# Chunked delta-rule attention with two MLP layers: first joins 64 rows at a time, a PSUM tile per engine in the first copies, low weight parts by GpSimd, ks of chunk 1 ahead of y

## The chip, the core and the metric

One Trainium2 chip, one of its cores. The metric is the device time of one execution in microseconds (us). The engines are named as in the profile: PE is TensorE's matmuls, PEld its weight loads, DVE is VectorE, ACT is ScalarE, POOL is GpSimd, SP is SyncE, which here issues nearly all DMAs.

## The reference

```python
def _attn_ref(q, k, v, beta):                 # (4, 8, 768, 48): batch, heads, tokens, head size
    k_n = k / (np.linalg.norm(k, axis=-1, keepdims=True) + 1e-06)
    state = np.zeros((B, H, D, D)); y = np.zeros_like(q)
    for t in range(S):
        kt, vt, bt = k_n[:, :, t], v[:, :, t], beta[:, :, t, None]
        y[:, :, t] = einsum('bhd,bhde->bhe', q[:, :, t], state)
        v_old = einsum('bhde,bhd->bhe', state, kt)
        state = state + bt[:, :, :, None] * einsum('bhd,bhe->bhde', kt, vt - v_old)
    return y
def _moe_ref(x, w_in, w_out):                 # 3072 tokens, 384 -> 2048 -> 384
    h = x @ w_in
    return np.where(h > 0, h, np.exp(np.minimum(h, 0)) - 1) @ w_out
def _moe2_ref(x, w_in, w_out):
    h = x @ w_in
    return (h / (1 + np.exp(-1.702 * h))) @ w_out
# reference: _moe2_ref(_moe_ref(attention as (3072, 384)))
```

All in float32.

## The kernel before, in words

**Attention.** The 768 tokens are cut into 12 chunks `c` of 64; two chunks make a pass `p`. The 32 sequences (4 batches, 8 heads) lie in two halves of the partitions, 16 each. Inside a chunk the token-by-token recurrence becomes a triangular system: `gram64` or `gram` multiplies the keys by themselves (into `z`), `inverse(p)` inverts the unit triangular 32x32 blocks on DVE (one step is a product, L318, and a sum, L323), `across` or the chunk's own `m1` and `m2` join the 32-blocks to 64. Passes 0 to 2 (`FINE`) run the steps on 16x16 blocks only, and `join16` joins two 16-blocks into a 32-block by two products on TensorE: `left` (L357, copied to `ys` by L359) and `right` (L368, subtracted by L371). Then a chunk runs `kq` (L455, masked by L466), `ks` (old state times keys, L513, subtracted from v by L518), `w` (L530), `state` (L549, copied by L765 and L767 in chunk 0, added by L556 later) and `y` (L574 and L584, split by L595 on ACT and L596 on DVE).

**MLP.** Every float32 operand is split into a high and a low word, and a product is three matmuls: high times high, high times low, low times high. A unit is one of 16 column blocks `m` of one pass of 512 tokens in one layer, 192 units in all. A unit `u` is `up` (9 matmuls of 128x128 by 128x512, L669), an activation (ACT L678 and L679, DVE L682), the split into `gh` (ACT L691) and `gl` (DVE L694), and, two units later, `down` (9 matmuls, L706). `up` needs a PSUM tile `h`, of which there are two: unit u waits until L682 of unit u-2 has read its own.

**Weights.** `prep` makes the two words of a weight tile out of its raw float32 form: a DMA, a power-of-two change on ACT (L628), `shift` (L635) and `rest` (L638) on DVE, `high` (L645, a cast on ACT) and `low` (L649, the difference of the bits and the high word, 128x768, on DVE). In layer 0 these run one or two units ahead of the unit that reads the tile.

**Order.** The kernel is scheduled by hand: each engine runs its instructions in the order of the program. `schedule` first writes out the prologue call by call: grams of chunks 0 and 1, whose copies out of PSUM (`diag`, L765 on ACT and L767 on DVE in turns, and `off`, L224 on ACT) fill `z`; the 16-steps of pass 0; grams of chunks 2 and 3; then the joins and the recurrences of chunks 0 and 1, with steps of pass 1 between (`also`). After `self.early = False` come the units. `fill`, `mid`, `end` and `tail` are tables by unit; in `fill` stands the weight preparation, and behind it the steps of later passes, which `spread` lays over the units by the room that `taken` leaves. Pass 2 has its steps in units 9 to 16.

**PSUM.** `ps_m` holds two `h` tiles and the three sums `acc0` to `acc2`, a bank each; `ps_a` holds `ps_w` (two banks in one tile, `wide()`) and one bank `ps_b`. `bank(True)` gives an `h` tile while `early` is set, `banks(i)` gives two of the sums.

Of the kernel before, what the change touches and what calls it, by code (L numbers as in the profile page):

```python
# [20 lines left out]
P = 128  # L21
# [11 lines left out]
class Kernel:  # L33
# [34 lines left out]
    def constants(self):  # L68
# [5 lines left out]
        self.ident = self.ap.tile([P, P], F32, name="ident")  # L74
        make_identity(nc, self.ident)
# [126 lines left out]
    def gram64(self, c, kt, ps):  # L202
# [10 lines left out]
        def diag(i, hf):  # L213
# [124 lines left out]

    def join16(self, c, home):
# [4 lines left out]
        own = {}  # L344

# [4 lines left out]
        def left(half):  # L350
# [3 lines left out]
            for u in range(8 * half, 8 * half + 8):  # L354
# [6 lines left out]
        def right(half):  # L361
# [3 lines left out]
            for u in range(8 * half, 8 * half + 8):  # L365
# [51 lines left out]
    def chunk(self, c):  # L417
# [123 lines left out]
        def state():  # L541
            if last:
                return
            ps = self.wide()
            for u in range(8):
                for hf, ab in self.order():
                    k = self.w_half(hf, ab)
                    t, r = self.tok(k), slice(64 * (1 - ab), 64 * (1 - ab) + D)
                    pe.matmul(ps[r, hf, ss(u)], g["kn"][t, hf, hs(u)], su[k][t, hf, ss(u)], start=True, stop=True)  # L549
            for hf, ab in self.order():  # L550
                k = self.w_half(hf, ab)
                r, q = [slice(64 * (1 - x), 64 * (1 - x) + D) for x in (k, ab)]
                if first:
                    self.evac(1 - hf, heads(nx[k][r, hf]), heads(ps[q, hf]))
                    continue
                v.tensor_tensor(out=heads(nx[k][r, hf]), in0=heads(su[k][r, hf]), in1=heads(ps[q, hf]), op=ALU.add)  # L556
# [49 lines left out]
    def prep(self, layer, ms, pools):  # L606
# [171 lines left out]
    def schedule(self):  # L778
# [66 lines left out]
        both = self.wide()  # L845
        diag0, off0, _ = self.gram64(0, self.grp[0]["kt"], [both[:, hf] for hf in range(2)])
        diag0(1, 0)
        self.load_q(0, gate=True)
        diag0(1, 1)
        diag1, off1, _ = self.gram64(1, self.grp[1]["kt"], self.banks(1))  # L850
        diag1(1, 0)
        diag1(1, 1)
        off0(0)
        off0(1)
        off1(0)
        off1(1)
# [6 lines left out]
        for f in first[0]:  # L863
            f()
        c0["kq"]()
        for c, kg in ((2, self.kg), (3, kg3)):
            both = self.wide()
            all_of = self.gram64(c, kg, [both[:, hf] for hf in range(2)])[2]
            all_of(0)
            all_of(1)  # L870
# [49 lines left out]
        for f in loads[4:6]:  # L920
            f()
        c0["y"]()
        c1["ks"]()
# [223 lines left out]
```

## Time and profile before

| | us |
|---|---|
| median of three runs (1002.73 to 1006.55) | 1005.05 |
| the profiled execution, as timed | 1009.37 |
| its span, first to last instruction | 1007.6 |
| PE busy in it | 952.0 |
| DVE busy | 598.0 |
| ACT busy | 444.6 |
| POOL busy | 49.4 |

The profile is of one execution. It gives each instruction's start and duration, groups them by line and shape, and puts an idle stretch of an engine down to the instruction that ended last before it (the releaser); "issue" means that the profile shows no releaser. Busy time of an engine is an average over stages: the first 75 us are attention alone, up to about 196 us the units share the engines with attention and weight preparation, and after that TensorE has almost no gaps.

### The profile page before, as it was taken

The numbers are of one execution on the slowest core, as the hardware profiler recorded it, in microseconds if no ns is written. First come the engines' busy times: TensorE is split into PE (matmuls) and PEld (weight loads), VectorE is DVE, ScalarE is ACT, GpSimd is POOL, SyncE is SP. The second block draws the span as 40 slices with busy tenths as digits, with TensorE's granted clock in tenths as the row PEclk, the third lists the DMA queues.
The fourth block names the chain that finished last, engine by engine and source line by source line (L and its number), as shares of the span: only waits on it lengthen the run. The fifth ranks groups of instructions, "written<-read, shape, count | busy, mean of one in ns | idle before, by whom it ended". The sixth has DMA issues, their size and how long they took to land.

```text
span 1007.6 us, 27118 instructions
## 1 busy us (share of the span) xinstructions
PE 952.0 (94%) x12288; PEld 780.1 (77%) x12288; DVE 598.0 (59%) x1054; ACT 444.6 (44%) x726; POOL 49.4 (5%) x55
## 2 busy tenths in 40 slices
PE   4678889899999999999999999999999999999998
PEld 3566667687877887888887888888888888888886
DVE  5969649857986888688344777744333333333333
ACT  5535455445345344444545776533333333333332
POOL 2100000001001001000000010100101001010000
PEclk9999889999999999999999999999999999999999
DMA  7144232402220321211101921001010010100000
GB/s 253 51 164 149 87 112 101 138 35 59 71 97 18 91 65 56 76 55 52 34 2 73 408 84 63 1 1 63 1 63 1 0 63 1 43 20 1 32 1 31
DMA packets 20180, 68.43 MB, mean 68 GB/s; under 512 B 3168, under 2 KB 4704, under 8 KB 20064
## 3 DMA queue, kind: packets, MB, share of 16 engines
q1 hardware_dynamic: 19920, 66.56, 19.1%
q8 instruction: 96, 1.57, 0.6%
q14 instruction: 20, 0.16, 0.1%
q10 hardware_dynamic: 144, 0.13, 0.0%
HBM read 57.25 MB, written 9.44 MB: 66 GB/s over the span
## 4 chain that ended last, share of the span: by engine, by line
PE 88%; DVE 8%; issue 3%; ACT 1%; DMA 0%; ACTq 0%; DVEq 0%
PE h L669 39%; PE acc L706 28%; PE accn L706 10%; PE ps_w L455 1%; PE ps_w L513 1%; PE ps_w L530 1%; PE ps_w L194 1%; PE ps_w L549 1%; PE ps_w L574 1%; PE ps_w L584 1%; DVE wt L649 1%; DVE tmp L318 1%; PE ps_b L368 1%; DVE W L323 1%; PE ps_w L408 1%
## 5 line engine op out<-in xcount | busy, mean ns | idle before, releaser
L669 PE MATMUL h<-xh,wt 128*128 128x512 f32 x1152 | 398.8, 401 | 6.3 <-DVE W L328 2.6
L706 PE MATMUL acc<-gh,wt 128*128 128x512 f32 x864 | 292.6, 393 | 0.5 <-DVE xo L767 0.5
L669 PEld LDWEIGHTS h<-xh,wt 128*128 128x128 f32 x1152 | 219.4, 191 | 56.2 <-DVE W L328 2.7
L669 PE MATMUL h<-xl,wt 128*128 128x512 f32 x576 | 227.8, 395 | 0.0
L691 ACT CAST gh<-t 128x512 fp32r<-128x512 f32 x192 | 119.4, 622 | 191.1 <-DVE t L682 134.9
L706 PEld LDWEIGHTS acc<-gh,wt 128*128 128x128 f32 x864 | 162.8, 188 | 35.9 <-issue 0.9
L694 DVE TENSOR_TENSOR gl<-t,gh 128x512 fp32r<-128x512 f32 x192 | 138.5, 722 | 71.5 <-ACT gh L691 71.3
L706 PE MATMUL acc<-gl,wt 128*128 128x512 f32 x432 | 168.7, 390 | 0.0
L688 DVE TENSOR_TENSOR t<-t,h 128x512 f32<-128x512 f32 x96 | 66.0, 687 | 168.8 <-ACT t L685 168.8
L685 ACT ACTIVATE t<-h 128x512 f32<-128x512 f32 x96 | 57.4, 598 | 187.3 <-PE h L669 187.3
L669 PEld LDWEIGHTS h<-xl,wt 128*128 128x128 f32 x576 | 110.0, 191 | 21.4
L682 DVE SCALAR_TENSOR_TENSOR t<-t,h 128x512 f32<-128x512 f32 x96 | 65.6, 683 | 79.6 <-ACT t L679 79.1
L678 ACT ACTIVATE t<-h 128x512 f32<-128x512 f32 x96 | 57.4, 598 | 98.1 <-PE h L669 97.9
L706 PE MATMUL accn<-gh,wt 128*128 128x512 f32 x288 | 96.5, 389 | 0.0
L706 PEld LDWEIGHTS acc<-gl,wt 128*128 128x128 f32 x432 | 81.5, 189 | 16.3
L706 PEld LDWEIGHTS accn<-gh,wt 128*128 128x128 f32 x288 | 54.1, 188 | 11.2
L679 ACT ACTIVATE t<-t 128x512 f32<-128x512 f32 x96 | 60.7, 632 | 3.1
L706 PE MATMUL accn<-gl,wt 128*128 128x512 f32 x144 | 56.0, 389 | 0.0
L733 POOL TENSOR_TENSOR xl<-x1r,xh 128x512 fp32r<-128x512 f32 x18 | 24.1, 1337 | 407.2 <-ACT xh L732 314.4
L466 DVE TENSOR_TENSOR x<-ps_w,mask_p 64x512 f32<-64x512 f32 x44 | 30.2, 687 | 9.7 <-PE ps_w L455 9.3
L638 DVE SCALAR_TENSOR_TENSOR w<-raw,w 128x768 uint32<-128x768 uint32 x32 | 33.7, 1053 | 0.9
L313 DVE TENSOR_TENSOR W<-W,tmp 128x30 f32<-128x30 f32 (+14 forms) x90 | 29.9, 332 | 3.1
(171 smaller groups left out, 804.4 us busy)
## 6 DMA issues: line engine op xcount, KB each, us to landing
raw<-in_w SPq DMA_DIRECT2D x32, 768.0 KB, 7.4
kt<-in_kT SPq DMA_DIRECT2D x12, 512.0 KB, 4.3
x<-in_qT SPq DMA_DIRECT2D x24, 256.0 KB, 4.1
kg<-in_kT SPq DMA_DIRECT2D x9, 512.0 KB, 4.8
kn<-in_kn SPq DMA_DIRECT2D x12, 384.0 KB, 3.0
x1d<-xo SPq DMA_DIRECT2D x12, 384.0 KB, 2.9
x1r<-x1d SPq DMA_DIRECT2D x6, 768.0 KB, 4.8
vn<-in_vn SPq DMA_DIRECT2D x11, 384.0 KB, 3.6
```

Source lines behind the costliest of these rows:

```text
L313: v.tensor_tensor(out=w, in0=w, in1=t, op=ALU.add)
L466: v.tensor_tensor(out=g["x"][k][self.tok(k), 8 * hf:8 * hf + 8], in0=i, in1=self.mask_p[t].unsqueeze(1).to_broadcast(list(i.shape)), op=AL ...
L638: v.scalar_tensor_tensor(out=bits[m], in0=words(m, 0), scalar=29, in1=bits[m], op0=ALU.logical_shift_right, op1=ALU.bitwise_or)
L669: nc.tensor.matmul(hps, wt[:, part, k * P:(k + 1) * P], src[:, k], start=(i == 0), stop=(i == 3 * NK - 1))
L678: nc.scalar.activation(out=t, in_=hps, func=AF.Relu, scale=-1.0)
L679: nc.scalar.activation(out=t, in_=t, func=AF.Exp, scale=-1.0)
L682: nc.vector.scalar_tensor_tensor(out=t, in0=t, scalar=-1.0, in1=hps, op0=ALU.add, op1=ALU.max)
L685: nc.scalar.activation(out=t, in_=hps, func=AF.Sigmoid, scale=1.702)
L688: nc.vector.tensor_tensor(out=t, in0=t, in1=hps, op=ALU.mult)
L691: nc.scalar.copy(gh, t)
L694: nc.vector.tensor_tensor(out=gl, in0=t, in1=gh.bitcast(F32), op=ALU.subtract)
L706: self.nc.tensor.matmul(self.acc[c], wt[:, part, DM + c * P:DM + (c + 1) * P], src, start=(m == 0 and i == 0), stop=(m == NM - 1 and i == 2),)
```

## The change

- `join16`: `left` for chunks 0 and 1 and `right` for chunk 1 multiply 64 rows at a time. The stationary operand is a 64x64 block-diagonal tile (`self.blocks`, two tiles of 128x1024, set to zero by POOL at the start), into which `block` copies the 16-blocks by four ACT copies of 32x16x16. A product of 16 heads is then 32 matmuls instead of 64.
- The first grams: chunk 0 uses two `h` banks instead of one two-bank tile; of each chunk's two tiles ACT copies one and DVE the other (`evac(1 - hf, ...)`), four copies each, where the two took turns on each tile. The `off` copies move behind the first four steps of pass 0 (`start`, `take`, `diag`, `root`), and chunk 3's gram gets banks of its own instead of `ps_w`.
- `state` of chunk 0 uses two `h` banks, one for ACT's and one for DVE's copies.
- `low` of layer 0 runs on POOL instead of DVE, and `taken` in its units is 0.37 instead of 0.6. The 16 `low`s of layer 1 stay on DVE.
- `ks` of chunk 1 stands ahead of `y` of chunk 0.
- The identity tile goes.

```diff
+        self.blocks = []
+        for c in range(2):
+            t = self.wp.tile([P, 2 * DM, 2], F32, name="raw", tag="wt").rearrange("p k i -> p (k i)")[:, 0:1024]
+            nc.gpsimd.memset(t, 0.0)
+            self.blocks.append(t.rearrange("p (u t) -> p u t", u=16))
...
-                    self.evac(i + far, z[r, :, 0:32], p[r, :, 32 * far:32 * far + 32])
+                    self.evac(1 - hf, z[r, :, 0:32], p[r, :, 32 * far:32 * far + 32])
...
+    def block(self, to, x):
+        for q in range(4):
+            r, i = slice(32 * q, 32 * q + 32), 32 * (q % 2)
+            self.nc.scalar.copy(to[r, :, i:i + 16], x[r, :, 0:16])
...
+        wide = [c < 2, c == 1]
+        def pairs(ps, x, half):
+            for u in range(8 * half, 8 * half + 8):
+                for o in (0, 64):
+                    r = slice(o, o + 64)
+                    pe.matmul(ps[r, u, :], own["d"][r, u, :], x[r, u, :], start=True, stop=True)
...
+            if wide[1]:
+                if half == 0:
+                    own["d"] = self.blocks[0]
+                    self.block(own["d"], own["t1"])
+                pairs(ps, own["ys"], half)
...
-            ps = self.wide()
+            if first:
+                ps = [self.bank(True) for _ in range(2)]
...
-            v.tensor_tensor(out=wt[:, 1], in0=bits.pop(m).bitcast(F32), in1=wt[:, 0].bitcast(F32), op=ALU.subtract)
+            (v if layer else nc.gpsimd).tensor_tensor(out=wt[:, 1], in0=bits.pop(m).bitcast(F32), in1=wt[:, 0].bitcast(F32), op=ALU.subtract)
...
-        for f in first[0]:
+        for f in first[0][:4]:
+            f()
+        for off in (off1, off0):
+            off(0)
+            off(1)
+        z = self.pas[0]["z"]
+        self.block(self.blocks[0], z[:, 0:16])
+        for f in first[0][4:-1]:
             f()
...
+        self.block(self.blocks[1], z[:, 16:32])
+        all3 = self.gram64(3, kg3, [self.banks(1)[1], self.bank()])[2]
...
+        c1["ks"]()
         c0["y"]()
-        c1["ks"]()
...
-            taken[m - 2] = 0.6
+            taken[m - 2] = 0.37
```

ACT's order at the very start, before; `acc_150` and `acc_151` are the two tiles of chunk 1's gram, `ps_w` that of chunk 0:

```order
L765 COPY z<-ps_w 32x8x32 x2
L155 COPY x_141<-one 128x1
L765 COPY z<-ps_w 32x8x32 x2
L765 COPY z<-acc_150 32x8x32 x2
L765 COPY z<-acc_151 32x8x32 x2
L224 COPY z<-ps_w 32x8x32 x4
L224 COPY z<-acc_150 32x8x32 x2
L224 COPY z<-acc_151 32x8x32 x2
L273 ACTIVATE nb<-dg 128x32
```

The same stretch of ACT after the change; `h` is chunk 0's first tile, `raw` the first block-diagonal tile:

```order
L793 COPY z<-h 32x8x32 x4
L157 COPY x_141<-one 128x1
L793 COPY z<-acc_150 32x8x32 x4
L275 ACTIVATE nb<-dg 128x32
L226 COPY z<-acc_150 32x8x32 x2
L226 COPY z<-acc_151 32x8x32 x2
L226 COPY z<-h 32x8x32 x4
L345 COPY raw<-z 32x16x16 x4
```

The square root (`nb`) moved ahead of the eight `off` copies, and four block copies follow them.

PE's order through the joins of chunks 0 and 1, before (L357 left, L368 right, L482 and L497 `m1` and `m2` of chunk 0):

```order
L357 MATMUL h<-xl,z 32x16 x64
L357 MATMUL ps_b<-xl,z 32x16 x32
L368 MATMUL h<-xh 32x16 x64
L357 MATMUL ps_b<-xl,z 32x16 x32
L482 MATMUL h<-z 32x32 x32
L368 MATMUL ps_b<-xh 32x16 x32
L497 MATMUL h<-xl,xh 32x32 x32
L368 MATMUL ps_b<-xh 32x16 x32
```

The same stretch after the change (L360 is the 64-row product, L392 the right product of chunk 0, L506 and L521 `m1` and `m2`):

```order
L360 MATMUL h<-xl,raw 64x16 x32
L360 MATMUL ps_b<-xl,raw 64x16 x16
L392 MATMUL h<-xh 32x16 x64
L360 MATMUL ps_b<-xl,raw 64x16 x16
L506 MATMUL h<-z 32x32 x32
L360 MATMUL ps_b<-xh,raw 64x16 x16
L521 MATMUL h<-xl,xh 32x32 x32
L360 MATMUL ps_b<-xh,raw 64x16 x16
```

The groups kept their places; 96 of 352 matmuls went. The last two L360 groups read a block tile that ACT fills between its copies of `m1` and of `m2`.

POOL's order from the start of the joins to pass 3, before (L490 and L399 clear parts of `z`, L263 masks `W` of an inverse):

```order
L490 MEMSET z 32x16x32 x4
L399 MEMSET z 32x32x32 x2
L263 AFFINE_SELECT W<-W 128x1024
L267 MEMSET W 128x16x16
L263 AFFINE_SELECT W<-W 128x1024
```

The same stretch after the change:

```order
L514 MEMSET z 32x16x32 x4
L677 TENSOR_TENSOR wt<-w,wt 128x768 x7
L423 MEMSET z 32x32x32 x2
L677 TENSOR_TENSOR wt<-w,wt 128x768 x5
L265 AFFINE_SELECT W<-W 128x1024
L269 MEMSET W 128x16x16
L677 TENSOR_TENSOR wt<-w,wt 128x768 x4
L265 AFFINE_SELECT W<-W 128x1024
```

Sixteen `low`s (L677) came to POOL; the masks and clears now stand in a row with them.

## Rows read from the trace of the kernel before

**Rows 1.** The page, busy time, share and instruction count of each engine.

```profile
PE 952.0 (94%) x12288; PEld 780.1 (77%) x12288; DVE 598.0 (59%) x1054; ACT 444.6 (44%) x726; POOL 49.4 (5%) x55
```

**Rows 2.** Stages: length, busy PE, PEld, DVE, ACT, POOL, granted clock, DMA.

```profile
75.00:92.50 17.50, 14.77 (x164) 10.37 (x164) 16.72 (x24) 8.81 (x15) 0.00 (x0) 0.90 0.43 147
92.50:150.00 57.50, 48.27 (x1394) 38.61 (x1393) 31.64 (x46) 30.30 (x51) 1.90 (x2) 0.88 0.32 108
150.00:196.00 46.00, 39.61 (x829) 31.60 (x827) 44.12 (x93) 24.04 (x38) 1.58 (x2) 1.00 0.41 131
196.00:1007.60 811.60, 805.50 (x8242) 659.47 (x8242) 452.60 (x770) 345.89 (x555) 35.44 (x29) 1.00 0.15 52
```

**Rows 3.** Timeline, first copies: start, length, instruction, [idle before <- releaser].

```profile
6.65 0.42 DVE L767 COPY z<-ps_w 32x256 f32<-32x256 f32 x1 [6.65 <-ACT z L765]
10.51 0.88 DVE L767 COPY z<-acc 32x256 f32<-32x256 f32 x2 [0.43 <-ACT z L765]
11.81 1.49 ACT L224 COPY z<-ps_w 32x256 f32<-32x256 f32 x4
12.28 1.90 DVE L257 STREAM_TRANSPOSE W<-z 128x1024 f32<-128x1024 f32 x1
14.47 1.27 POOL L263 TENSOR_SCALAR_AFFINE_SELECT W<-W 128x1024 f32<-128x1024 f32 x1 [8.70 <-DVE dg L262]
```

**Rows 4.** Timeline, joins to the first unit, 40 to 75 us.

```profile
40.39 0.42 DVE L371 TENSOR_TENSOR z<-xl,h 128x256 f32<-128x256 f32 x1
48.84 1.96 PE L530 MATMUL acc<-vn,z 64*64 64x48 f32 x64
56.47 1.12 DVE L767 COPY su<-ps_w 48x384 f32<-48x384 f32 x2 [1.50 <-ACT su L765]
57.11 0.66 PE L574 MATMUL h<-x,su 128*32 128x64 f32 x16
61.83 0.33 PE L584 MATMUL h<-x,su 128*32 128x64 f32 x4 [2.06 <-issue]
66.18 2.08 PE L530 MATMUL acc<-raw,z 64*64 64x48 f32 x64 [1.17 <-DVE raw L518]
74.77 0.80 PE L669 MATMUL h<-xh,wt 128*128 128x512 f32 x1 [0.98 <-DVE xl L596]
```

**Rows 5.** PE's waits in 75 to 200 us, and the instruction queue of the page.

```profile
PE ps_w L455 <- issue: 2.9, 1, 2.9
PE h L669 <- DVE W L328: 2.6, 1, 2.6
PE ps_w L194 <- ACT z L411: 2.2, 1, 2.2
PE ps_w L194 <- issue: 2.1, 1, 2.1
PE ps_w L408 <- issue: 2.0, 1, 2.0
PE h L669 <- DVE wt L649: 1.5, 1, 1.5
PE h L669 <- DVE t L682: 1.2, 1, 1.2
q8 instruction: 96, 1.57, 0.6%
```

**Rows 6.** A stretch of 2.5 us at the lower clock, columns as in rows 2.

```profile
117.50:120.00 2.50, 2.50 (x48) 2.19 (x43) 1.18 (x2) 0.00 (x0) 0.00 (x0) 0.50 0.02 7
```

**Rows 7.** POOL beside DVE in layer 1, the same DVE line alone, and `low`.

```profile
588.98 1.29 POOL L733 TENSOR_TENSOR xl<-x1r,xh 128x512 fp32r<-128x512 f32 x1 [6.86 <-ACT xh L732]
589.13 1.95 DVE L638 SCALAR_TENSOR_TENSOR w<-raw,w 128x768 uint32<-128x768 uint32 x1
78.82 0.96 DVE L638 SCALAR_TENSOR_TENSOR w<-raw,w 128x768 uint32<-128x768 uint32 x1
L649 DVE TENSOR_TENSOR wt<-w,wt 128x768 fp32r<-128x768 f32 x32 | 30.3, 951 | 0.0
```

More of the change, by code (lines that the diff above doesn't have):

```diff
@@ L7 @@
 from concourse import mybir
-from concourse.masks import make_identity
 F32 = mybir.dt.float32
@@ L353, in left @@
             ps = own["ps"]
-            for u in range(8 * half, 8 * half + 8):
+            if wide[0]:
+                own["d"] = self.blocks[c]
+                pairs(ps, s["zt"][:, us, 16:32], half)
+            for u in range(8 * half, 8 * half + 8 * (not wide[0])):
                 for q in range(4):
@@ L364, in right @@
             ps = own["ps"]
-            for u in range(8 * half, 8 * half + 8):
+            if wide[1]:
[3 more added lines that the diff above has]
+                pairs(ps, own["ys"], half)
+            for u in range(8 * half, 8 * half + 8 * (not wide[1])):
                 for q in range(4):
@@ L543, in state @@
                 return
-            ps = self.wide()
+            if first:
+                ps = [self.bank(True) for _ in range(2)]
+            else:
+                both = self.wide()
+                ps = [both[:, hf] for hf in range(2)]
             for u in range(8):
@@ L548, in state @@
                     t, r = self.tok(k), slice(64 * (1 - ab), 64 * (1 - ab) + D)
-                    pe.matmul(ps[r, hf, ss(u)], g["kn"][t, hf, hs(u)], su[k][t, hf, ss(u)], start=True, stop=True)
+                    pe.matmul(ps[hf][r, ss(u)], g["kn"][t, hf, hs(u)], su[k][t, hf, ss(u)], start=True, stop=True)
             for hf, ab in self.order():
@@ L553, in state @@
                 if first:
-                    self.evac(1 - hf, heads(nx[k][r, hf]), heads(ps[q, hf]))
+                    self.evac(1 - hf, heads(nx[k][r, hf]), heads(ps[hf][q]))
                     continue
-                v.tensor_tensor(out=heads(nx[k][r, hf]), in0=heads(su[k][r, hf]), in1=heads(ps[q, hf]), op=ALU.add)
+                v.tensor_tensor(out=heads(nx[k][r, hf]), in0=heads(su[k][r, hf]), in1=heads(ps[hf][q]), op=ALU.add)
         def y():
@@ L844, in schedule @@
         self.a_start(0)
-        both = self.wide()
-        diag0, off0, _ = self.gram64(0, self.grp[0]["kt"], [both[:, hf] for hf in range(2)])
-        diag0(1, 0)
+        diag0, off0, _ = self.gram64(0, self.grp[0]["kt"], [self.bank(True) for _ in range(2)])
+        diag0(0)
         self.load_q(0, gate=True)
-        diag0(1, 1)
+        diag0(1)
         diag1, off1, _ = self.gram64(1, self.grp[1]["kt"], self.banks(1))
[L851 to L856, printed above, removed]
+        diag1(0)
+        diag1(1)
         self.load_kg(2)
@@ L862, in schedule @@
         self.load_kg(3, kg3)
-        for f in first[0]:
+        for f in first[0][:4]:
[6 more added lines that the diff above has]
+        for f in first[0][4:-1]:
             f()
         c0["kq"]()
[L866 to L870, printed above, removed]
+        both = self.wide()
+        all2 = self.gram64(2, self.kg, [both[:, hf] for hf in range(2)])[2]
+        all2(0)
+        all2(1)
+        self.block(self.blocks[1], z[:, 16:32])
+        all3 = self.gram64(3, kg3, [self.banks(1)[1], self.bank()])[2]
+        all3(0)
+        all3(1)
+        first[0][-1]()
         self.load_v(0)
```

4 lines of the change are left out of this document (1 added, 3 removed).

## The prediction

> **What bounds the kernel now.** I read the page's busy line first, then stages, then timelines and waits inside the stages. TensorE (PE) is busy 94% of the span [rows 1], but unevenly: after 196 us it works 805.5 of 811.6 us, so there nothing but its own work counts, and it idles 2.7 us between 75 and 92.5, 9.2 from there to 150 and 6.4 from there to 196 [rows 2]. Up to 75 us PE runs only small products. The end moves by what the prologue (up to the first L669 at 74.77 [rows 4]) and the idle time between 75 and 196 us give back. Who is late differs: in 150 to 196 DVE is busy 44.1 of 46 us, in 92.5 to 150 only 31.6 of 57.5 [rows 2]. Between 75 and 200 us the largest single waits of PE are "issue": 2.9, 2.1 and 2.0 us before small products; one of 2.6 stands under DVE W L328 [rows 5]. In rows 4 L584 waits 2.06 us for "issue" as well.
>
> What "issue" is can be worked out. The instruction queue moved 96 packets, 1.57 MB [rows 5]; PE and PEld have 24,576 records [rows 1], which is 96 x 256. Counted along PE's program, each of these stalls begins at record 191 + 256k (k = 10 for L584, 16, 19 and 22 for the three, 31 for the 2.6). A float32 product of 48 columns takes four records, so small products use up 256 records in little more than a microsecond, faster than the next packet comes; among large products (0.2 us for two records, from 805.50 us for 8242 [rows 2]) nothing shows. So the number of PE instructions costs time, even where they are short. [...]
>
> **The change, part by part.** The profiled execution took 1009.37 us with a span of 1007.6, 4.3 above the median of 1005.05; I sum against the former and take the sum off the median.
>
> *First copies.* DVE's pair of 0.88 us waited 0.43 for ACT, and the transpose came at 12.28 [rows 3]. Its first copy began at 6.65, when ACT's first of about the same 0.42 was done, and one in two waited again. With a tile each, both engines start together at about 6.25, and eight DVE copies of 0.44 run without a partner: transpose at about 9.9, **-2.4**. I count nothing for the square root, moved ahead of the `off` copies (1.49 on ACT): the inverse starts from POOL's L263, which ends at 15.74 and is released by DVE's L262 [rows 3].
>
> *Joins.* 96 of 352 products go, but PE is not late there: the copies and subtractions on DVE are (L371 at 40.39 has no idle time of DVE before it [rows 4]). I cost PE's saving at 0; DVE's subtractions and masks hide it, and if they did not, 96 products of four records, some 1.3 us per 256 at best, would give up to 2. The block tiles are cleared by POOL, which idles for 8.70 us at that time [rows 3]. The identity tile and the other banks of chunk 3's gram cost nothing that is waited for. The four block copies (4 x 0.37 on ACT, from `off` at 1.49 for four) stand ahead of the copy of `m2`'s result and part of `right` of chunk 1. So of the 2.4 gained, w of chunk 0 (48.84 [rows 4]) keeps about 1.3.
>
> *State copies.* L767 waited 1.50 for ACT's half of one tile [rows 4]. With two banks that goes: L767 ends at about 54.7 instead of 57.59, **-2.9** including the 1.3.
>
> *ks ahead of y.* At 54.7 ks comes first, 64 products of 48 columns like L530's 1.96 us [rows 4], ending near 56.7. Behind it on PE stands y. It ran from 57.11 to about 63.05 (66.18 less the wait of 1.17 and ks's 1.96), 5.9 us with L584's stall of 2.06 [rows 4], so 3.9 of work, and a stall again if a packet boundary falls in it: end 60.6 to 62.6. Meanwhile DVE subtracts (L518), which before put 1.17 us on the path [rows 4] and now lies under y; at worst it waits for two `low`s on POOL (1.94 each, below) and ends at 60.6, so even that is covered. w of chunk 1 starts at 60.6 to 62.6 instead of 66.18, and needs as before 8.6 us to the first L669. That gives 3.6 to 5.6; with the two terms above in it, the prologue is worth **-4.7** (bounds -3 to -5.5; y's copies on ACT now wait behind ks).
>
> *Units 0 to 3 (75 to 92.5).* The wait for L649 (1.5) goes to POOL, which runs `low` right after the cast and 1.5 units before its use, and a part of L682's 1.2 [rows 5], since DVE, 16.7 of 17.5 us busy [rows 2], sheds 0.95 per `low`. With PE's idle time goes one half-clock stretch (1.7). DVE's chain gives 0.8 back. **-3.1** (-1 to -3.9).
>
> *Fetch stalls.* 384 records fewer, and two waits more, shift every later boundary by one and a half packets. Of the stretches of 256 records after it, those with small products alone stall some 2 us, that with 4 large ones about 1, with 14 about 0.5 (a large product fills 0.2 us, and beside 18 of them no stall showed). The list of after has one full stall (in L392 to L196), 1 and 0.5, and one that hides under the 2.2 us wait for L411; the 2.0 and the 2.6 [rows 5] have no counterpart. Before: 2.9 + 2.1 + 2.0 + 2.6 = 9.6; after: about 3.6 to 5.6, and a half-clock stretch less or more. **-4.0** (0 to -7).
>
> *150 to 196 us.* Here DVE ends last. Six `low`s (0.95 each [rows 7]) leave it, -5.7. But POOL's operations hold up DVE ones that read two operands from SBUF: L638 takes 0.96 alone and 1.95 beside a POOL operation of 1.29 that started 0.14 earlier [rows 7]. `low` on POOL, 768 columns instead of 512, takes an estimated 1.94. Five of them (units 9 to 13) would put 9.7 on DVE if all its operations were blocked; those that read PSUM are not, which spares some 0.4 each: +7.7. Net **+2.0** (-5.7 to +4). `taken` at 0.37 only moves six 16-steps from units 14 to 16 to 10 to 13. [...]
>
> *Units 0 to 8.* The same blocking, with DVE idle nearly half the time [rows 2]: **+0.5**. A `low` late on POOL would hold `shift` two units on; there are two units of slack. POOL's masks and clears stand behind `low`s but are due later. SP's loads of x for the second chunk wait for y as before, those of the keys move earlier; nothing waits for either.
>
> Sum: -4.7 - 3.1 - 4.0 + 2.0 + 0.5 = -9.3. 1009.4 becomes 1000.1, the median 1005.05 about **996**.
>
> **The rivals.** *The lock decides (slower).* Every one of the 14 `low`s up to unit 13 holds DVE for 1.94, where DVE is on the path throughout: 27.2 less the 13.3 that leave it is +13.9; PE's idle time behind it brings three half-clock stretches, +5.1. With -10.3 from prologue and fetch stalls the time is about 1013.5. For it: L638 doubles [rows 7], DVE is 44.1 of 46 busy. Against: in 92.5 to 150 DVE is idle 26 us [rows 2], and only part of its operations read SBUF twice. It decides from the point at which a `low` costs PE over 1.1 us net.
>
> *The stalls stay (same).* Boundaries fall on other small products, as long as before, and the half-clock stretches with them: the fetch term is 0, the rest -5.3, time about 1000; with the prologue at its lower bound 1002. For it: there are as many small products in units 1 to 9 as there were. Against: the counted list. [...]
>
> *No lock (faster).* DVE's work in these units reads PSUM or finds its gaps, as most POOL operations now pass without a trace of harm: term 150 to 196 at -5.2, units 0 to 8 at 0, sum -17, time 988. For it: POOL is 5% busy and has room. Against: rows 7.
>
> **How the numbers follow.** Forecast (994 to 999) 0.55; the lock 0.10; same 0.18; no lock 0.17. A measurement of this kernel tells about 0.5% (5 us) from no change. Faster by more than that, below 1000: the forecast and the no-lock case nearly whole, 0.70; slower, 0.10; the remainder of 0.20 is the rival at 1000 to 1002 and the forecast's upper end. The range goes from the no-lock case, 987, to 1005, past the same rival, and leaves out the lock and the tail of the no-lock case.
>
> **What would show it.** The transpose (L259) at about 9.9; the first L697 near 70; no 1.5 wait before DVE's state copy; POOL's L677 at 1.94 each and two-operand DVE operations stretched beside it in units 9 to 13; "issue" stalls at other lines than L455 and L408, and three or four half-clock stretches instead of five. A first L697 later than 72 shows the prologue wrong; DVE without a stretched operation shows the lock wrong; PE waits of 2 us for DVE in units 9 to 16 would show that its price is too small; stalls of the same sum fell the fetch term.

## The result, and the profile of the changed kernel

| | before | changed |
|---|---|---|
| median of five runs (lowest to highest), us | 1006.55 (1002.73 to 1014.42) | 996.09 (993.81 to 998.32) |
| profiled execution, as timed, us | 1009.37 | 997.16 |
| its span, us | 1007.6 | 995.4 |

The ratio is 0.9884, with a 95% interval of 0.9834 to 0.9934; a second set of runs (below, e9) gave 0.9879, 0.9865 to 0.9893. The kernel became faster by 1.2% (no change lies outside the interval), and 996.09 us stands beside the 996 of the forecast. The medians differ by 10.5 us, the two profiled executions by 12.2; the forecast's sum was 9.3. That it is so near is in part luck, as the parts show.

The page of the changed kernel: its busy line, and two groups of its costliest instructions (line, engine, operation, count, then busy us and mean ns of one).

```profile
PE 953.3 (96%) x12096; PEld 782.7 (79%) x12096; DVE 597.4 (60%) x1038; ACT 449.1 (45%) x738; POOL 81.3 (8%) x71
L666 DVE SCALAR_TENSOR_TENSOR w<-raw,w 128x768 uint32<-128x768 uint32 x32 | 38.3, 1196 | 0.9
L677 POOL TENSOR_TENSOR wt<-w,wt 128x768 fp32r<-128x768 f32 x16 | 30.5, 1912 | 66.9 <-ACT wt L673 66.8
```

Against [rows 1] PE has 192 matmul records and as many weight loads fewer, 384 together, as counted. (The two lists of PE's order in "The change" add up to 320 and 224 matmuls: 96 of 320 went, not of 352; nothing was worked out from the 352.) DVE has lost sixteen instructions of 0.95 us (16 x 0.95 = 15.2) and is busy for 597.4 instead of 598.0 us: most of the relief came back in other instructions (below, under e2).

To see where the time went, both traces are cut where the same work ends: before the first up product, after 293 matmul records of PE, after 1262 more, and where 8242 are left. Columns as in [rows 2]. The kernel before:

```profile
74.80:94.00 19.20, 16.47 (x293) 11.80 (x293) 18.38 (x26) 8.81 (x15) 0.00 (x0) 0.91 0.45 158
94.00:149.00 55.00, 45.77 (x1261) 36.57 (x1260) 29.41 (x42) 29.30 (x49) 1.90 (x2) 0.88 0.29 97
149.00:196.00 47.00, 40.61 (x846) 32.41 (x835) 44.89 (x94) 25.04 (x39) 1.58 (x2) 1.00 0.42 137
```

The changed kernel:

```profile
72.00:88.50 16.50, 14.20 (x293) 10.79 (x293) 15.51 (x22) 8.79 (x15) 4.97 (x3) 1.00 0.47 152
88.50:139.00 50.50, 44.87 (x1262) 35.48 (x1261) 30.79 (x38) 29.37 (x49) 12.72 (x9) 0.90 0.35 117
139.00:185.00 46.00, 42.10 (x832) 33.81 (x833) 42.12 (x87) 24.55 (x39) 12.69 (x8) 0.96 0.38 127
185.00:995.40 810.40, 804.02 (x8242) 657.79 (x8240) 454.01 (x771) 346.04 (x556) 35.47 (x29) 1.00 0.15 52
```

The prologue gave 2.8 us (74.8 to 72.0), the first stage 2.7 (19.2 to 16.5), the second 4.5, the third 1.0 and the rest 1.2 (811.6 [rows 2] to 810.4): 12.2 in all. The last two belong together, since the wait at 193 us of the kernel before and the half-clock stretch behind it straddle the cut: 2.2.

From the first up product to the end both kernels have the same 10,624 matmul records, but PE was busy with them for 908.4 us before and for 905.2 after (add up PE's busy time over the rows, with 805.50 from [rows 2]). So 3.2 of the 12.2 us are no wait at all: less of the time stood at the lower clock, a granted clock of 0.50 (two stretches of 3.4 us fewer, below, each worth half its length, 3.4 in all).

PE's waits in the units of the changed kernel, by what ended them:

```profile
PE ps_w L612 <- issue: 3.7, 1, 3.7
...
PE ps_w L196 <- issue: 1.7, 1, 1.7
PE ps_b L376 <- issue: 1.2, 1, 1.2
PE acc L734 <- issue: 1.1, 1, 1.1
PE h L697 <- DVE t L710: 1.0, 1, 1.0
```

The waits for DVE's `low` (1.5 in [rows 5]) and the "issue" waits at kq, at 2.9, and at L408, now L432, are gone; new ones of 3.7 us at y of unit 9 (L612) and of 1.2 at L376 stand in their place. Stretches of 3.4 us at the granted clock of 0.50 between 80 and 205 us number four, against six before (one row of 6.8 counted as two).

By cause the two profiled executions compare as follows; e9 is the changed kernel once more. Waits are those of up to 205 us, and the 2.6 us at L669 [rows 5] counts as "issue", since it stands at a packet boundary.

| us | before | changed | e9 |
|---|---|---|---|
| first up product starts | 74.8 | 72.1 | 73.4 |
| from there: PE's waits for DVE | 6.5 | 1.2 | 5.4 |
| "issue" waits | 9.6 | 8.7 | 6.0 |
| PE busy | 908.4 | 905.2 | 902.5 |

From before to changed that is 2.7, 5.3, 0.9 and 3.2 us. The one kernel in two executions of nearly equal length has its time in different places, so the size of a single part can't be read from one execution to better than some 4 us.

### Where the prologue's gain went

The transpose came at 9.93 us, 2.4 earlier, as worked out. DVE kept those 2.4 us up to 44.7 us (L304 at 44.71; its counterpart ran at 47.06 before). Then, in the changed kernel, on ACT, PE and DVE (start, length, instruction, [idle before <- releaser]), with the transpose ahead of them and the start of `ks` and of the first up product behind:

```profile
9.93 1.90 DVE L259 STREAM_TRANSPOSE W<-z 128x1024 f32<-128x1024 f32 x1
40.57 1.16 ACT L510 COPY xl<-h 32x512 f32<-32x512 f32 x2 [2.50 <-PE h L506]
42.28 1.65 ACT L345 COPY raw<-xh 32x256 f32<-32x256 f32 x4
43.15 0.39 PE L360 MATMUL ps_b<-xh,raw 64*64 64x16 f32 x2 [2.62 <-ACT raw L345]
49.58 0.42 DVE L395 TENSOR_TENSOR z<-xl,ps_b 128x256 f32<-128x256 f32 x1 [2.68 <-PE ps_b L360]
49.17 0.34 PE L554 MATMUL acc<-vn,z 64*64 64x48 f32 x2
56.88 1.96 PE L537 MATMUL ps_w<-su,kt 48*64 48x48 f32 x64
72.07 0.80 PE L697 MATMUL h<-xh,wt 128*128 128x512 f32 x1 [1.01 <-DVE xl L624]
```

ACT idles 2.50 us, waiting for m1's product, copies it, and only then fills the block tile for chunk 1's right products (L345), though their operand was ready before: in e1 the same copies run at 32.35 us. PE, whose order puts these products ahead of m2, waits 2.62 us for them, DVE 2.68 us behind PE. So w of chunk 0 (L554) starts at 49.17 us, later than the 48.84 of [rows 4].

### The profile page after: what moved, and what is told of

Read it like the earlier page. It is cut to its first block, busy times and chain, and to the rows that moved or that the text cites. A ratio compares the mean times of both kernels' runs of the same rounds, so it can differ in the third digit from the quotient of the medians.

```text
span 995.4 us, 26765 instructions
## 1 busy us (share of the span) xinstructions
PE 953.3 (96%) x12096; PEld 782.7 (79%) x12096; DVE 597.4 (60%) x1038; ACT 449.1 (45%) x738; POOL 81.3 (8%) x71
## 4 chain that ended last, share of the span: by engine, by line
PE 92%; DVE 5%; issue 2%; ACT 1%; DMA 0%; ACTq 0%; DVEq 0%
PE h L697 40%; PE acc L734 30%; PE accn L734 10%; PE ps_w L537 1%; PE ps_w L196 1%; PE ps_w L479 1%; PE ps_w L554 1%; PE ps_w L602 1%; PE ps_w L612 1%; PE ps_w L577 1%; PE ps_w L432 1%; PE ps_b L376 1%; PE ps_b L392 0%; DVE W L325 0%; DVE tmp L320 0%
## 5 line engine op out<-in xcount | busy, mean ns | idle before, releaser
L734 PE MATMUL acc<-gh,wt 128*128 128x512 f32 x864 | 293.4, 394 | 1.7 <-issue 1.1
L734 PEld LDWEIGHTS acc<-gh,wt 128*128 128x128 f32 x864 | 163.4, 189 | 37.9 <-issue 2.8
L722 DVE TENSOR_TENSOR gl<-t,gh 128x512 fp32r<-128x512 f32 x192 | 139.5, 727 | 71.4 <-ACT gh L719 71.3
L734 PE MATMUL acc<-gl,wt 128*128 128x512 f32 x432 | 169.3, 392 | 0.0
L710 DVE SCALAR_TENSOR_TENSOR t<-t,h 128x512 f32<-128x512 f32 x96 | 65.7, 685 | 74.2 <-ACT t L707 73.7
L706 ACT ACTIVATE t<-h 128x512 f32<-128x512 f32 x96 | 57.4, 598 | 97.8 <-PE h L697 97.4
L734 PE MATMUL accn<-gh,wt 128*128 128x512 f32 x288 | 96.4, 389 | 0.0
L734 PEld LDWEIGHTS acc<-gl,wt 128*128 128x128 f32 x432 | 81.6, 189 | 16.4
L734 PEld LDWEIGHTS accn<-gh,wt 128*128 128x128 f32 x288 | 54.1, 188 | 11.3
L734 PE MATMUL accn<-gl,wt 128*128 128x512 f32 x144 | 56.0, 389 | 0.0
L666 DVE SCALAR_TENSOR_TENSOR w<-raw,w 128x768 uint32<-128x768 uint32 x32 | 38.3, 1196 | 0.9
L677 POOL TENSOR_TENSOR wt<-w,wt 128x768 fp32r<-128x768 f32 x16 | 30.5, 1912 | 66.9 <-ACT wt L673 66.8
L490 DVE TENSOR_TENSOR x<-ps_w,mask_p 64x512 f32<-64x512 f32 x44 | 30.2, 686 | 6.9 <-PE ps_w L479 6.4
```

The costliest lines, as they stand in the source:

```text
L490: v.tensor_tensor(out=g["x"][k][self.tok(k), 8 * hf:8 * hf + 8], in0=i, in1=self.mask_p[t].unsqueeze(1).to_broadcast(list(i.shape)), op=AL ...
L666: v.scalar_tensor_tensor(out=bits[m], in0=words(m, 0), scalar=29, in1=bits[m], op0=ALU.logical_shift_right, op1=ALU.bitwise_or)
L677: (v if layer else nc.gpsimd).tensor_tensor(out=wt[:, 1], in0=bits.pop(m).bitcast(F32), in1=wt[:, 0].bitcast(F32), op=ALU.subtract)
L706: nc.scalar.activation(out=t, in_=hps, func=AF.Relu, scale=-1.0)
L710: nc.vector.scalar_tensor_tensor(out=t, in0=t, scalar=-1.0, in1=hps, op0=ALU.add, op1=ALU.max)
L722: nc.vector.tensor_tensor(out=gl, in0=t, in1=gh.bitcast(F32), op=ALU.subtract)
```

## The experiments

In the versions of e1, e6, e7 and e10 lines from 388 on stand one lower than in the changed kernel (L394 for L395), and those from 365 to 384 one higher (L377 for L376). All ratios are to the kernel before in the same set of runs.

### e1: the block copies earlier

```diff
+            self.t1[c] = own["t1"]
...
             if wide[1]:
-                if half == 0:
-                    own["d"] = self.blocks[0]
-                    self.block(own["d"], own["t1"])
+                own["d"] = self.blocks[0]
...
         j0[2]()
+        self.block(self.blocks[0], self.t1[1])
         conv[0]()
```

> The changed kernel with one edit: the four ACT copies that fill the block tile from chunk 1's turned triangle stand right behind the copy of chunk 0's left product, where ACT idles 2.2 us, instead of behind ACT's copies of m1. Theory (the block copies gave the prologue's gain back: DVE's L395 of chunk 1 waited 2.68 us for right products that waited 2.62 for the copies): w of chunk 0 starts at about 46.5 us instead of 49.2, the first up product at about 69.4 instead of 72.1, total 2 to 3 us below the changed kernel, about 993.5. Rival (a PE instruction packet or ACT's own order is the limit there, the copies only show it): w of chunk 0 moves by less than 0.7 us and the total by less than 0.7.

Measured: 991.42 us (990.8 to 992.37), ratio 0.9852, 0.9833 to 0.9871. The places, in the trace of e1:

```profile
32.35 1.64 ACT L345 COPY raw<-xh 32x256 f32<-32x256 f32 x4
40.54 1.89 PE L360 MATMUL ps_b<-xh,raw 64*64 64x16 f32 x32
45.73 0.34 PE L553 MATMUL acc<-vn,z 64*64 64x48 f32 x2
47.03 0.42 DVE L394 TENSOR_TENSOR z<-xl,ps_b 128x256 f32<-128x256 f32 x1
68.54 0.50 PE L696 MATMUL h<-xh,wt 128*128 128x512 f32 x1 [1.21 <-DVE xl L623]
```

No wait stands before L360 and none before L394; w of chunk 0 is 3.4 us earlier (45.73 against 49.17) and the first up product 3.5 (68.54 against 72.07). The theory holds: the place of four copies in ACT's order cost what the first copies had brought. Of the 3.5 us at the first up product only 2.2 are left at w of chunk 1 (62.00 against 64.20); the other 1.3 come from the products of y behind it, whose groups of 16 records took 0.41 us and followed each other by 0.22 in e1, where they took 0.65 and followed by 0.43 in the changed kernel, which is not the copies' doing. This version has the lowest ratio of all; its interval still touches that of the changed kernel (0.9865 to 0.9893 in e9).

### e8: without the 64-row products

```diff
-        wide = [c < 2, c == 1]
+        wide = [False, False]
...
         diag1(1)
+        ps = self.bank()
+        for i in range(32):
+            nc.tensor.matmul(ps[0:64, 16 * (i % 32):16 * (i % 32) + 16], self.mask_p[0:64, :], self.mask_p[0:64, 0:16], start=True, stop=True)
...
-        self.block(self.blocks[0], z[:, 0:16])
...
-        self.block(self.blocks[1], z[:, 16:32])
```

> The changed kernel without the 64-row products: left and right of chunks 0 and 1 as in the kernel before, no block copies on ACT; and 32 needless products behind the gram of chunk 1, so that the packet boundaries fall as in the changed kernel. Theory (the 64-row joins are worth nothing on the path by themselves, DVE hides PE's saving, and their block copies are what took 2.4 us): w of chunk 0 starts at about 46.5 us instead of 49.2, total 2 to 4 us below the changed kernel, 992 to 994. Rival (fewer products shorten the joins): w of chunk 0 at 49 or later, total 996 or more.

Measured: 994.56 us (990.26 to 1000.72), ratio 0.9883, 0.9849 to 0.9916. In its trace w of chunk 0 and the subtraction that waited:

```profile
44.47 0.42 PE L554 MATMUL acc<-vn,z 64*64 64x48 f32 x2
46.82 0.42 DVE L395 TENSOR_TENSOR z<-xl,ps_b 128x256 f32<-128x256 f32 x1
```

w starts 4.7 us earlier with 96 products more, and L395 without a wait; it is 1.3 us earlier than in e1, too, which has the products and the copies out of the way. In the joins, then, the 64-row products are worth nothing on the path, as the prediction had it, and cost what their block copies hold up. The first up product starts at 69.43 us, 2.6 earlier than in the changed kernel. In the total the gain doesn't show: the profiled execution, at 990.26, is the lowest of five, and the ratio is that of the changed kernel, where 2 to 4 us were expected.

### e5: y ahead of ks again

```diff
-        c1["ks"]()
         c0["y"]()
+        c1["ks"]()
```

> The changed kernel with ks of chunk 1 again behind y of chunk 0: that part alone is undone. Theory, the prediction's step (ks first lets DVE's subtraction hide under y): ks starts some 5.4 us later, DVE's L542 lies open between ks and w, w of chunk 1 starts 1.5 to 3 us later than 64.2 and the first up product at 73.5 to 75; total 1.5 to 3.5 us above the changed kernel, 997.5 to 999.5. Rival (y's own copies on ACT and DVE are what the first up product waits for, so the order of ks and y is without effect): first up product within 0.5 us of 72.1, total within 1 us of 996.

Measured: 999.1 us (995.71 to 1002.2), ratio 0.9907, 0.9879 to 0.9934. In its trace:

```profile
63.40 0.84 PE L537 MATMUL ps_w<-su,kt 48*64 48x48 f32 x42 [2.23 <-issue]
65.38 2.08 PE L554 MATMUL acc<-raw,z 64*64 64x48 f32 x64 [1.14 <-DVE raw L542]
72.91 0.50 PE L697 MATMUL h<-xh,wt 128*128 128x512 f32 x1 [1.22 <-DVE xl L624]
```

DVE's subtraction lies open again (1.14), w of chunk 1 starts at 65.38 instead of 64.20, the first up product at 72.91 instead of 72.07. So the mechanism is there, at about 1 us, less than the 1.5 to 3 expected; an "issue" stall stands in either order (2.23 in ks here, 1.60 in y of the changed kernel), so even that 1 us isn't the order's alone. The total is some 3 us above by the ratio, but its interval touches that of e9, and what the rest of it is isn't shown.

### e2 and e11: `low` on POOL, undone and alone

e2 is the changed kernel with that part undone:

```diff
-            (v if layer else nc.gpsimd).tensor_tensor(out=wt[:, 1], in0=bits.pop(m).bitcast(F32), in1=wt[:, 0].bitcast(F32), op=ALU.subtract)
+            v.tensor_tensor(out=wt[:, 1], in0=bits.pop(m).bitcast(F32), in1=wt[:, 0].bitcast(F32), op=ALU.subtract)
...
-            taken[m - 2] = 0.37
+            taken[m - 2] = 0.6
```

> The changed kernel with low of layer 0 back on DVE and taken back at 0.6: that part alone is undone. Theory from the trace of after (POOL's lock takes back about three quarters of DVE's relief, all where DVE has room, and none on PE's path): waits of PE for DVE return, 1.5 us on a low in the first units and some 3 between units 11 and 15; total 3 to 6 us above the changed kernel, 999 to 1002. Rival, the prediction's step (the lock costs 2 us net in units 9 to 16 and 0.5 before, the first units gain 2 to 3): total 0 to 1 above the changed kernel, 996 to 997.

Measured: 997.03 us (994.44 to 1000.32), ratio 0.9905, 0.9887 to 0.9923. PE's waits for DVE in the units:

```profile
PE h L697 <- DVE wt L677: 3.6, 2, 2.1
PE ps_w L196 <- DVE xl L624: 1.5, 1, 1.5
PE ps_w L602 <- DVE su L584: 1.3, 2, 1.1
PE ps_w L554 <- DVE vn L542: 0.7, 1, 0.7
```

e11 makes the opposite edit in the kernel before, so that PE's records stay as they were.

> The kernel before with one part of the change alone: low of layer 0 on POOL, and taken at 0.37; PE's records and their packet boundaries stay where they were. Theory from the traces so far (DVE sheds 15 us and gets 11 to 13 back, PE waits for DVE less by 1.5 in the first units and by 1 between units 11 and 15; the prologue loses nothing): total 1 to 4 below the kernel before, ratio 0.996 to 0.999. Rival, the prediction's step for these units: -1.5 and +2.5, total 0 to 1.5 above the kernel before.

Measured: 1005.21 us (1001.89 to 1008.65), ratio 0.9968, 0.9951 to 0.9986. PE's waits for DVE in the units:

```profile
PE ps_w L530 <- DVE vn L518: 2.2, 1, 2.2
...
PE h L669 <- DVE t L682: 0.8, 1, 0.8
```

Undone, the waits on `low` and on the later DVE work return (3.6, 1.5, 1.3, 0.7); alone, the wait on `low` goes, and between units 10 and 15 one wait of 2.2 replaces those that sum to 3.5 in e2's rows without the first. The wait of 2.7 for L710 in unit 1, which e9 has, is not in e2, so of the 3.6 on `low` some 0.9 is net. The ratios put the part at some 2.6 us (0.9905 against e9's 0.9879) and 3.2 us (1 less 0.9968). No gain at all lies outside e11's interval, and its total is where the theory had it. e2's interval touches that of the changed kernel, and its median, 0.9 us above 996.09, is where the rival had it; by itself e2 decides nothing.

What POOL costs DVE can be read in one pair of the changed kernel, POOL's operation and DVE's next to it:

```profile
83.61 2.11 POOL L677 TENSOR_TENSOR wt<-w,wt 128x768 fp32r<-128x768 f32 x1 [3.57 <-ACT wt L673]
84.04 2.50 DVE L666 SCALAR_TENSOR_TENSOR w<-raw,w 128x768 uint32<-128x768 uint32 x1
```

and in two groups of e2, where `low` is on DVE:

```profile
L666 DVE SCALAR_TENSOR_TENSOR w<-raw,w 128x768 uint32<-128x768 uint32 x32 | 33.7, 1053 | 0.9
L663 DVE TENSOR_SCALAR w<-raw 128x768 uint32<-128x768 uint32 x32 | 17.8, 556 | 5.5 <-ACT raw L656 4.2
```

against the L666 of the changed kernel above and this:

```profile
L663 DVE TENSOR_SCALAR w<-raw 128x768 uint32<-128x768 uint32 x32 | 21.7, 677 | 6.2 <-ACT raw L656 4.2 <-POOL wt L677 0.7
```

L666 starts 0.43 us after POOL and ends 0.82 us after it, and takes 2.50 us where the same operation takes 0.96 alone [rows 7]: it stood still beside POOL. With POOL's `low`s L666 costs 4.6 us more in sum, L663 3.9, L325 1.6 (11.8 for 10.2), L320 1.5 (11.7 for 10.2) and L722 0.9 (139.5 for 138.6): 12.5 us for 16 `low`s, 0.8 each. Operations with an operand in PSUM were not stretched: L710 has a mean of 685 ns for 684, L584 553 for 553. So the lock is real, but met few of DVE's operations here.

### e4 and e3: only the packet boundaries moved

e4 is the kernel before with 32 products that nobody reads (the loop shown under e8), so that its boundaries fall at the content at which they fall in the changed kernel.

> The kernel before with the same 32 needless products on PE behind the gram of chunk 1, so that its packet boundaries fall at the content at which they fall in the changed kernel. Theory (boundaries set the issue stalls): 2.9 at L455, 2.0 at L408 and 2.6 at L669 go; about 3.7 at an L584 of unit 9, 1.2 at L357, 1.7 at L194 and 1.1 at L706 come; half-clock stretches fall from six to about four; total 2 to 5 us below the kernel before. Rival (places and data): the old stalls stay, total within 1 us of before.

Measured: 1000.7 us (995.52 to 1004.38), ratio 0.9938, 0.9917 to 0.996: 5.6 us less, by work that is of no use. PE's "issue" waits in the units:

```profile
PE ps_w L194 <- issue: 2.5, 1, 2.5
PE acc L706 <- issue: 1.8, 1, 1.8
PE ps_b L395 <- issue: 0.7, 1, 0.7
```

They sum to 5.0. Before they were 9.6 with the 2.6 at L669 ([rows 5]), and 10.2 in e11, which has the same records; the waits at L455, L408 and L669 are gone. Of those expected anew L194 and L706 came, larger (2.5 for 1.7, 1.8 for 1.1), L357 and L584 did not; L395 stood in no list. PE's busy time from the first up product on fell as well, from 908.4 to 903.0 us, with four stretches at the lower clock instead of six. That the boundaries do it is borne out by the places of the stalls; how much of the clock's part is theirs isn't shown.

e3 is the converse, the changed kernel with the same 32 products.

> The changed kernel with 32 needless float32 products of 16 columns (128 records) on PE behind the gram of chunk 1, where PE idles; nothing reads them. They move every later packet boundary back to the content at which it fell before the change. Theory (boundaries set the issue stalls): stalls of about 2.9 at kq (L479 as numbered in the changed kernel), 2.0 at L432, 2.1 at L196 and 2.6 at an up product around unit 15 come back; those of 3.7 at L612, 1.2 at L376 and 1.1 at L734 go; two more half-clock stretches; total 2 to 5 us above the changed kernel, 998 to 1001. Rival (the stalls belong to places and data, not to the count): the same lines stall as in the changed kernel, total within 1 us of 996.

Measured: 999.89 us (995.12 to 1004.79), ratio 0.9931, 0.9904 to 0.9958. PE's "issue" waits in the units:

```profile
PE ps_w L196 <- issue: 6.1, 2, 4.4
```

The total rose as expected (by 5 us against e9's ratio of 0.9879). The waits at L612, L376 and L734 went, and that at L196 came back, at 4.4 us, with a second of 1.7 at the place of the 2.6 of before; but the waits at kq and at L432 did not return, and the sum of "issue" waits, 6.1 us against 6.0 in e9, doesn't explain the rise. In these runs the boundary decided where a stall began (every "issue" wait of the units named here begins at a record 191 + 256k), not alone how long it was.

Part of the rest is in the instruction queue. The time from PE's passing of one boundary to the start of the next packet, worked out from the records of that queue, with the DMA share of that stretch:

```
boundary        kernel    passed    packet starts   lag    DMA share   stall after it
6847            changed   164.67    165.46          0.8    0.00        none
7359            changed   174.24    175.20          1.0    0.00        none
6079 (unit 9)   changed   138.90    144.80          5.9    0.73        3.7
6079 (unit 9)   e1        135.16    140.46          5.3    0.73        3.1
6079 (unit 9)   e10       138.71    144.12          5.4    0.77        3.4
6079 (unit 9)   e2        139.20    140.72          1.5    0.85        none
6079 (unit 9)   e9        139.59    140.64          1.1    1.0         none
```

With the DMA engines idle (share 0.00) the packet started 0.8 and 1.0 us after the boundary. In unit 9, while weights and keys are loaded, it took 5.3 to 5.9 us in three executions, which then stalled for 3.1 to 3.7 us, and 1.5 and 1.1 us in two with the same boundary, which did not. One of these, e9, is the changed kernel itself, so the edit doesn't decide it; nor does the load of the DMA engines, which was higher where the packet came early. Why it waited in some and not in the others is open.

### e9: the changed kernel once more

> The changed kernel itself once more, unedited, so that it and the next two share one chip and its runs of the kernel before. Theory (the time of one execution depends on where the half-clock stretches and the packets fall, the work being the same): median 995 to 998, with the first up product at 70.5 to 72.5, and the 3.7 us stall at y of unit 9 present or not; where it is not, PE waits some 2.2 us for DVE's L542 in unit 11. Rival (that stall is fixed by the record count): it is there again at 3 us or more.

Measured: 996.91 us (996.06 to 998.92), ratio 0.9879, 0.9865 to 0.9893.

```profile
64.54 0.33 PE L612 MATMUL h<-x,su 128*32 128x64 f32 x9 [3.25 <-issue]
73.36 0.50 PE L697 MATMUL h<-xh,wt 128*128 128x512 f32 x1 [1.05 <-DVE xl L624]
...
PE ps_w L196 <- issue: 3.1, 1, 3.1
PE h L697 <- DVE t L710: 2.7, 1, 2.7
PE ps_w L554 <- DVE vn L542: 2.2, 1, 2.2
...
PE ps_w L602 <- issue: 1.3, 1, 1.3
```

The first up product starts at 73.36, later than expected: the stall in the prologue's y, 1.60 us in the execution above, is 3.25 here. The 3.7 at L612 in unit 9 is not there, and DVE's 2.2 in unit 11, which it had covered, is. The same holds across the runs with `low` on POOL: the three with that stall (the changed kernel, e1, e10) don't have the 2.2, the seven without it (e3, e5 to e9, e11) do. The total is the same within 1 us. So the stall was no fixed cost of the change, and where it falls away another wait takes its place.

### e6 and e7: other boundaries for the version of e1

30 and 39 of the same needless products in e1.

> The kernel of the early block copies (991.4) with 30 needless float32 products (120 records) on PE behind the gram of chunk 1. Theory (boundaries set the issue stalls): counted against that kernel's trace, with a stall of 3.3 us less the time that the 256 records before a boundary need, the stalls after the prologue rise by 5 us in sum and seven of them instead of four are long enough to bring a half-clock stretch of 1.7; total 7 to 12 above, 998 to 1003. Rival (what matters is only the one large stall at y of unit 9, which hangs on DMA traffic): that stall goes, total 988 to 991.

Measured: 999.75 us (990.92 to 1001.05), ratio 0.9901, 0.9867 to 0.9935. Against e1's ratio some 5 us more, less than expected. The "issue" waits in the units sum to 9.7 us against 6.4 in e1, 3.3 more where 5 were counted, among them 2.3 at L478, 2.0 at L431 and 1.4 at an up product; stretches at the lower clock number seven, as expected, against five in e1.

> The kernel of the early block copies (991.4) with 39 needless float32 products (156 records) on PE behind the gram of chunk 1. Theory (boundaries set the issue stalls): by the same count the stalls after the prologue fall to about 5.9 us in four places, and the one at y of unit 9 goes; total 1 to 4 us below, 987.5 to 990.5, with nine products more than the kernel that carries 30 of them and some 10 us less. Rival (the time follows the amount of needless work): both versions with needless products differ by less than 1 us.

Measured: 997.36 us (989.16 to 1002.07), ratio 0.9886, 0.9847 to 0.9925: not below e1, and not apart from e6 beyond the intervals. Its profiled execution, at 1002.07 the longest of six, shows 9.1 us of "issue" waits in the units where 5.9 were counted:

```profile
PE ps_w L196 <- issue: 4.4, 2, 2.6
```

They stand in five places, where the count had four. A count of records with one latency for every packet (3.3 us, the author's estimate) doesn't foretell these sums; this theory falls as a means of prediction, and only the place of the stalls is left of it.

### e10: three steps behind L709

```diff
-            spread(fill, 0, 2, [f for _, f in beside], [size for size, _ in beside])
+            spread(end, 0, 2, [f for _, f in beside], [size for size, _ in beside])
```

in the version of e1.

> The kernel of the early block copies (991.4) with the last three steps of pass 1's inverse on DVE (3.4 us: L329, L330, L336) behind L709 of unit 0 instead of ahead of it. Theory (PE's 2.64 us wait in unit 1 hangs on this order alone): the wait falls below 1 us with its half-clock stretch, total 1 to 4 below that kernel, 987.5 to 990.5. Rival (DVE has no room in units 0 to 3, the wait only moves to the next unit): the waits in units 0 to 3 keep their sum of 2.6 within 0.7, total 990.5 to 992.5.

Measured: 994.99 us (994.05 to 997.9), ratio 0.9863, 0.9844 to 0.9882, not below e1's 0.9852.

```profile
PE acc L733 <- DVE gl L721: 1.5, 1, 1.5
...
PE h L696 <- DVE W L329: 0.9, 1, 0.9
```

The wait of 2.7 in unit 1 shrank to 0.9, and 1.5 came at L733: 2.4 in sum. The rival holds: DVE has no room in the first units and the wait moves on. With the stalls at boundaries PE now waits for 6.8 us up to 100 us instead of 5.1.

## Why the prediction came out right

By its own steps, each against the stretch of the two profiled executions in which it lies:

| step | forecast | measured in its stretch |
|---|---|---|
| prologue | -4.7 | -2.8 |
| units 0 to 3 | -3.1 | -2.7 |
| fetch stalls and units 0 to 8 | -4.0 + 0.5 | -4.5 |
| units 9 to 16 and what straddles their end | +2.0 | -2.2 |
| sum | -9.3 | -12.2 |

The third row flatters the fetch term: its stalls lie in all three stretches behind the prologue. They fell by 3.6 us in this one and rose by 1.2 (L376) and 1.1 (3.7 at L612 for 2.6 at L669) in the other two.

- **First copies.** The transpose came at 9.93 for 9.9. Right.
- **Joins.** This step failed. It let 1.3 us of the 2.4 arrive at w of chunk 0; w came 0.3 later than before. The four copies' 1.65 us was known; that they stand behind ACT's copy of m1, and so behind PE's m1, was read from ACT's order as a length and not as a wait. e1 gives 3.4 us back. That PE's saving hides under DVE was right: e8 has it the other way, 96 products more and w earlier.
- **State copies.** No wait stands before DVE's copy, which ended at 56.33 instead of 54.7: the joins' error of 1.6 carried on. ks started later still, at 56.88, right behind m2 of chunk 1 on PE (L521, 55.03 to 56.95), which the step had not counted.
- **ks ahead of y.** y took 5.4 us with a stall of 1.6, within the 3.9 to 5.9 that were given, and DVE's two blocked steps (1.86 and 1.77 us, L325 and L320) stayed under it. The mechanism is right, at about 1 us (e5). The first up product started at 72.07 instead of near 70, later than the 72 that was to show the prologue wrong, and at 73.36 in e9.
- **Units 0 to 3.** The size came out, by other reasons. PE's idle time there fell by 0.4 us alone (2.7 to 2.3): the waits for DVE fell by 1.7, the wait on `low` among them, but an "issue" stall of 1.2 came at L376. The other 2.3 are PE's busy time (16.47 to 14.20), the clock's part, forecast at 1.7. That was the author's estimate for one stretch at the lower clock, which no row of the trace before gives as such; the same estimate is behind the 5.1 of the lock rival. What the runs showed is stretches of 3.4 us at 0.50, half of which is 1.7, each starting, in the trace before, within 1.6 us of the end of a wait of PE of 1.5 us or more, and in this stage a granted clock of 0.91 before and 1.00 after, 19.2 x 0.09 = 1.7 us. And the wait for DVE returns: of the executions with `low` on POOL (but for e10, whose order differs), the three whose first up product took 0.79 or 0.80 us (the changed kernel, e7, e11) wait 0.8 to 1.0 us in unit 1 for L709, L710 or L682, the six where it took 0.50 (e1, e3, e5, e6, e8, e9) wait 2.7 or 2.8. DVE is the bound there, and e10 shows that order doesn't change it.
- **Fetch stalls.** This term is mis-sized. It had the "issue" waits fall from 9.6 to between 3.6 and 5.6; they came to 8.7 in the profiled execution, near the equal sum that was to fell the term, and to 6.0 in e9. Of the list, L196, L734 and L419 came near the sizes given (1.7, 1.1 and 0.7, in sum 3.5); the 1.2 at L376 and the 3.7 at L612, each with nine large products among the 256 records ahead of it, did not stand in it, and e9 lacks both. That the boundaries matter was right: moved alone, they are worth 5.6 us in the kernel before (e4), clock included.
- **150 to 196 us.** This step failed: the sign was wrong. It took 1.55 us per `low` from the most blocked pair of [rows 7] for five of them; over all sixteen it is 0.8, less than the 0.95 that leaves DVE. In this stretch DVE's busy time fell from 44.89 to 42.12 us, so of the 5.7 that six `low`s took off it some 2.9 came back for five on POOL, 0.6 each, and PE's waits for DVE between units 10 and 15 (3.5 before) came to 0.2. `low` on POOL took 1.91 us, as estimated (1.94). The rival without a lock, at -5.2, was wrong as well: the lock is there (2.50 us for L666 beside POOL, 0.96 alone). e11 puts the whole part at 3.2 us gained, and e2, less surely, at 2.6.

Two workings in the rivals and in the reading of rows do not come out, and neither enters the sum. The -10.3 of the lock rival is called prologue and fetch stalls, which are -8.7; with that its time would be 1015.3. And 805.50 us for 8242 matmul records is 0.10 us a record, small and large ones mixed; large products follow each other by about 0.23 us at a granted clock of 1.00 (before, nine of L669 in 2.05 us from 110.48).

So a prologue forecast 1.9 us too good, and a fetch term some 3 us too good in this execution, stand against a DVE stage 4.2 us too bad and a clock that gave 3.2 us for the 1.7 put down. That these cancel is luck. The gain of the medians was 1.2 us larger than forecast (10.5 for 9.3), and the base 1.5 higher (1006.55 for 1005.05), so the median came out at 996. All five runs, 993.81 to 998.32, lie in the range of 987 to 1005.

What the runs show by themselves are two parts: the boundaries at 5.6 us (e4) and `low` on POOL at 3.2 (e11), each to about 2 us. With the 1.4 to 2.8 that the prologue gave (e9 and the changed kernel) that makes 10.2 to 11.6 beside the measured 10.5. The first copies and the state copies were not undone one by one; their part is read from the traces.

## What to carry to other kernels

When a step gets a new operand that another engine must first write, look at what stands ahead of that write in the writer's order, not at its length: four short copies cost the whole gain of the part beside them, and moving them brought w of chunk 0 3.4 us forward. A new lock between two engines is priced by the share of operations that it meets, which a trace gives as counts by operand, not by the worst pair (0.8 us per `low` here, for the 1.55 taken from that pair). And where small matmuls run in long rows, needless instructions can make a kernel faster (5.6 us in e4) by moving the packet boundaries, so a gain of 0.5% in such a kernel says little of the edit until the boundaries are held still.

## What was not expected of the hardware

- A DVE operation with a single operand in SBUF was blocked too: L663 (TENSOR_SCALAR, 0.556 us alone) took 2.15 us when it started just behind a `low` on POOL (at 121.85 us of the changed kernel).
- An instruction packet started 0.8 and 1.0 us after the two boundaries at which the DMA engines idled. While they loaded weights it was seen to start 1.1 to 5.9 us after one, and the share of the DMA engines' time in use did not tell which (0.73 to 0.77 for the long lags, 0.85 and 1.0 for the short).
- The first up products took 0.80 and 0.63 us up to 75.9 us in the changed kernel, where e1's took 0.50 and 0.39 from the start. The granted clock of the profile has no row ahead of 75.8 us there. In e7, where it has, the same products take 0.79 and 0.63 us at a granted clock of 0.50 (columns as in [rows 2]):

```profile
63.50:76.50 13.00, 10.13 (x200) 8.01 (x204) 7.50 (x16) 1.86 (x5) 0.00 (x0) 0.50 0.47 106
72.21 0.79 PE L696 MATMUL h<-xh,wt 128*128 128x512 f32 x1 [0.99 <-DVE xl L623]
```

So by their lengths the first up products of the changed kernel ran at 0.50, as did those of the kernel before (0.80 us [rows 4]).
